# Rows of V at 160 bytes instead of 130, value matmuls of 66 columns, and the mask's key pattern in a shared buffer

## The chip, the core and the metric

The kernel runs on one core of one Trainium2 chip. The metric is the device time of one launch in microseconds; lower is better.

## The reference

Two layers, one behind the other: attention with a block mask, and a gated feed-forward network (FFN) with RMS normalisation.

```python
# q, k, v: (4, 8, 768, 64) float32; blocks of 32, 24 blocks
scores = q @ k.T / sqrt(64)
mask = neighbouring blocks | first and last block (rows and columns) | 3 sampled blocks per row block
attn = softmax(where(mask, scores, -1e9))
x = (attn @ v), heads side by side        # (3072, 512)
xn = x / sqrt(mean(x * x) + 1e-6) * rms_g
out = (silu(xn @ w_gate) * (xn @ w_val)) @ w_out   # d_ff 1536
```

## The kernel before, in words

**Groups.** The 3072 tokens are worked through in nine groups of token tiles of 128: batch 0 in three groups of two tiles, batches 1 to 3 in two groups of three tiles each. For each group the loop runs over the 8 heads. A head has two steps:

- `scores` (matmuls in L325): keys times queries into PSUM, keys on the partitions, then one exponential per part on ACT (L328) into `ex` in bf16. The mask is part of the matmul: 64 rows of a head's K and Q, and 24 more rows that hold the key pattern (`kind`) and the query pattern (`qmask`).
- `values` (L336): for each token tile `it` and each of the six key tiles `jt` one matmul with a block of `ex` as the weights and a row of V as the moving operand, summed over `jt` in PSUM. `pv` (or `pv_two` for the first group, which takes two heads at a time) then multiplies the 64 columns by the reciprocal of the column of sums.

The values of a head are issued some heads behind its scores (`late_pv`), so that the exponentials are there.

**V.** `load_v` brings V of two heads to SBUF in float32 (`vraw`), and `cast_v` (L118, on DVE) writes it as bf16 into `Vp`, one of two tiles, by the parity of the batch. A partition of `Vp` holds 8 x 6 rows of `VW` = 65 elements: 64 of V, and a one that L204 sets once at the start, so that column 64 of the product is the sum of the exponentials. The rows lie end to end, 130 bytes each: row 6 h + jt belongs to head h and key tile jt.

**FFN.** When a group's attention is done, its rows are normalised and turned, and its FFN is cut into pieces (`ffn_pieces`: `gate` L436, `val` L447, `down` L464). `position()` puts them between the steps of the next group's heads at a fixed rate, so PE has matmuls of both at any time. The products of gate and value go to `hps`, which has two buffers in turn. The last group's FFN has no attention beside it.

**Batch changes.** K and Q of batch 0 are transposed on PE (L288). From batch 1 on they are transposed by DMA: `turn` (L301, into `turned`) and `place` (L310, into `KT` and `QT`), both issued on SP's queue, where the stores of the output (L471) are too.

**The mask's key pattern.** `ki_i` (L185, 32 x 768 int32) is written by GpSimd at the start. `mask_keys` (L224) reads it twice in the opening and turns it into `kind`.

**What sets the order.** Everything is issued in the order in which the Python code emits it; there is no scheduler that reorders. Waits between engines follow from the tiles.

Of the kernel before, what the change touches and what calls it, by code (L numbers as in the profile page):

```python
# [10 lines left out]
BF16 = mybir.dt.bfloat16  # L11
I32 = mybir.dt.int32
# [6 lines left out]
def kernel(  # L19
# [18 lines left out]
    P = 128  # L38
    B, H, S, D = q.shape
    NB = S // 32  # L40
    NC = S // P
# [12 lines left out]
    FIRST = NC // 2  # L54
    KR = D + NB
    NP = H // 2
    VW = D + 1

    ctx.enter_context(tc.manual_schedule())

    const = ctx.enter_context(tc.tile_pool(name="const", bufs=1))
    persist = ctx.enter_context(tc.tile_pool(name="persist", bufs=1))
    ld = ctx.enter_context(tc.tile_pool(name="ld", bufs=1))
    work = ctx.enter_context(tc.tile_pool(name="work", bufs=1))
# [19 lines left out]
    def load_one(b, pr, store):  # L84
        src, name = (k, "kbf") if store is kbf else (q, "qbf")
        t = ld.tile([P, 2, NC * D], BF16, name=name, tag=name, bufs=4)
        nc.gpsimd.dma_start(  # L87
            out=t,
            in_=src[b, 2 * pr:2 * pr + 2].rearrange("e (p c) d -> p e (c d)", p=P))
        store[(b, pr)] = t  # L90
# [21 lines left out]

    KT = [persist.tile([P, H, S], BF16, name=f"KT{i}") for i in range(2)]
    QT = [persist.tile([P, H, S], BF16, name=f"QT{i}") for i in range(2)]
    Vp = [persist.tile([P, H, NC, VW], BF16, name=f"Vp{i}") for i in range(2)]

    def cast_v(b, pr, eng):
        eng.tensor_copy(  # L118
# [63 lines left out]
    ident32 = const.tile([P, P], FP32, name="ident32")  # L182
    make_identity(nc, ident32)
    load_one(0, 1, kbf)
    ki_i = const.tile([32, S], I32, name="ki_i")  # L185
    nc.gpsimd.iota(ki_i[0:NB, :], pattern=[[1, NC], [NC, P]], base=0,
                   channel_multiplier=-32)
    for pr in range(NP):
# [14 lines left out]
    for i in range(2):  # L203
        nc.vector.memset(Vp[i][:, :, :, D:VW], 1.0)  # L204
    kc = const.tile([32, 1], FP32, name="kc")
# [126 lines left out]
    def values(grp, h, ex, op):  # L332
        b, c0, n = grp
        for it in range(n):
            for jt in range(NC):
                nc.tensor.matmul(  # L336
                    out=op[:, it, 0:VW], lhsT=ex[:, jt, it * P:(it + 1) * P],
                    rhs=Vp[b % 2][:, h, jt, :], start=(jt == 0), stop=(jt == NC - 1))

    def pv(grp, h, ex, stage):  # L340
        n = grp[2]
        op = ps_o.tile([P, HC, 80], FP32, name="op", tag="ot")
        values(grp, h, ex, op)
        rz = work.tile([P, HC], FP32, name="rz", tag="rz", bufs=2)
        nc.vector.reciprocal(out=rz[:, 0:n], in_=op[:, 0:n, D])  # L345
        nc.vector.tensor_tensor(  # L346
            out=stage[:, 0:n, h * D:(h + 1) * D], in0=op[:, 0:n, 0:D],
            in1=rz[:, 0:n].unsqueeze(2).to_broadcast([P, n, D]), op=ALU.mult)
# [3 lines left out]
    def pv_two(grp, h, ex, stage):  # L352

        if h % 2 == 0:
            pair_op[0] = ps_o.tile([P, 2, 2, 80], FP32, name="op2", tag="ot")
        op = pair_op[0]
        values(grp, h, ex, op[:, h % 2])
        if h % 2 == 0:
            return
        rz = work.tile([P, 2, 2], FP32, name="rz2", tag="rz2", bufs=2)  # L360
        nc.vector.reciprocal(out=rz, in_=op[:, :, :, D])
        nc.vector.tensor_tensor(  # L362
            out=stage[:, 0:2, (h - 1) * D:(h + 1) * D].rearrange("p c (e d) -> p e c d", e=2),
            in0=op[:, :, :, 0:D], in1=rz.unsqueeze(3).to_broadcast([P, 2, 2, D]), op=ALU.mult)
# [318 lines left out]
    for gi, grp in enumerate(groups):  # L683
        if gi == 0:
            continue
        b, c0, n = grp
# [101 lines left out]
```

## Time and profile before

| what | value |
|---|---|
| time, median of 3 runs | 314.73 us (314.66 to 314.91) |
| span of the profiled execution, first to last instruction | 312.8 us |
| median of the runs above that span | 1.9 us |
| PE busy | 302.8 us, 97% of the span |
| DVE, ACT, POOL busy | 202.7, 205.1 and 52.9 us |
| granted TensorE clock | 1.000 |
| value matmuls (L336) | 1152 |

For the profiled execution the profile gives the span; what lies outside of it is taken from the runs. The page of the profile lists busy times, the costliest groups of instructions by line, and the chain of waits that ended last. PE's matmuls are pipelined and their ends are modelled, so the busy times of groups overlap; the distance from one start to the next is what a matmul takes of PE's time. In the lines, "op<-Vp,ex" names the tile that is written and those that are read, "128x65" the moving operand (partitions x elements), and "idle before" the time in which the engine had nothing to do ahead of it, with what ended it.

### The profile page before, as it was taken

The page shows a single profiled execution, that of the slowest core. Times are in us where ns is not written, and L with a number is a line of the kernel's source. Part 1 is how long each engine was busy: PE and PEld are TensorE (multiplying, and loading weights), DVE is VectorE, ACT ScalarE, POOL GpSimd, SP SyncE. Part 2 cuts the span into 40 slices and gives each one's busy share as a digit, 9 for nine tenths or more (in the row PEclk, how much of TensorE's full clock was granted, in tenths as well). Part 3 has the DMA queues.
Part 4 walks back from the last instruction along what each step waited for, and adds up shares of the span by engine and source line. Part 5 has one row for each costly group of instructions (what it writes and reads, how often), then busy time and mean ns, then how long its engine had stood idle before and what let it go on. Part 6 is the DMA issues. An engine that isn't in the chain of part 4 may idle for free.

```text
span 312.8 us, 7261 instructions
## 1 busy us (share of the span) xinstructions
PE 302.8 (97%) x2850; PEld 201.1 (64%) x2869; DVE 202.7 (65%) x557; ACT 205.1 (66%) x332; POOL 52.9 (17%) x79
## 2 busy tenths in 40 slices
PE   8888999999999999999999999999999999999996
PEld 5666886976787566655666566655666566655653
DVE  6978875775578647682767457683777636674860
ACT  4976775777788586667676766766767567632331
POOL 9935132100220122012010122010000100010000
PEclk9999999999999999999999999999999999999999
DMA  7999999999789469605784277714000130002002
GB/s 166 271 210 208 208 265 142 175 227 136 209 147 162 104 134 158 141 20 146 149 152 101 70 182 127 143 40 119 34 2 0 36 118 2 1 2 101 2 0 102
DMA packets 66730, 36.84 MB, mean 118 GB/s; under 512 B 48308, under 2 KB 62288, under 8 KB 66696
## 3 DMA queue, kind: packets, MB, share of 16 engines
q0 software_dynamic: 16064, 17.90, 31.7%
q1 hardware_dynamic: 50596, 18.47, 27.7%
q8 instruction: 22, 0.36, 0.5%
q14 instruction: 12, 0.10, 0.1%
q10 hardware_dynamic: 36, 0.01, 0.0%
HBM read 28.59 MB, written 6.29 MB: 112 GB/s over the span
## 4 chain that ended last, share of the span: by engine, by line
PE 86%; DMA 7%; ACT 3%; DVE 2%; issue 1%; SPq 1%; ACTq 0%
PE yp L464 19%; PE gp L436 19%; PE vp L447 18%; PE st L325 18%; PE op L336 11%; DMA turned<-qbf 4%; ACT ex L328 2%; DMA QT<-turned 2%; DMA first<-in_q_dram 1%; PE tx L418 0%; DVE QT L293 0%; DVE junk L369 0%; DVE stage L362 0%; PE tqk L288 0%; SPq L133 0%
## 5 line engine op out<-in xcount | busy, mean ns | idle before, releaser
L328 ACT ACTIVATE ex<-st 128x768 bf16<-128x768 f32 x192 | 153.9, 812 | 56.2 <-PE st L325 54.5
L325 PE MATMUL st<-QT,KT 88*128 88x384 bf16 (+1 forms) x432 | 93.5, 308 | 1.9 <-DMA QT<-turned 0.7
L451 DVE SCALAR_TENSOR_TENSOR u<-th,gp 128x384 bf16<-128x384 bf16 (+1 forms) x108 | 54.8, 508 | 40.7 <-ACT th L440 39.0
L436 PE MATMUL gp<-xg,wg 128*128 128x384 bf16 (+1 forms) x432 | 80.7, 307 | 0.0
L447 PE MATMUL vp<-xg,wv 128*128 128x384 bf16 (+1 forms) x432 | 80.2, 307 | 0.4 <-DVE u L451 0.4
L464 PE MATMUL yp<-wo,hps 128*128 128x512 bf16 (+1 forms) x284 | 71.6, 369 | 0.9
L440 ACT ACTIVATE th<-gp 128x384 bf16<-128x384 f32 (+1 forms) x108 | 48.9, 453 | 28.9 <-PE gp L436 28.7
L453 DVE TENSOR_TENSOR hps<-u,vp 128x384 bf16<-128x384 bf16 (+1 forms) x108 | 55.1, 510 | 11.4 <-PE vp L447 0.3
L325 PEld LDWEIGHTS <-KT 88*128 88x128 bf16 x432 | 41.7, 98 | 27.0 <-issue 1.9
L447 PEld LDWEIGHTS <-wv 128*128 128x128 bf16 x432 | 40.6, 97 | 20.9 <-issue 0.6
L436 PEld LDWEIGHTS <-wg 128*128 128x128 bf16 x432 | 40.2, 97 | 20.3
L336 PEld LDWEIGHTS <-ex 128*128 128x128 bf16 x1152 | 46.0, 98 | 11.2 <-DVE stage L362 0.8
L336 PE MATMUL op<-Vp,ex 128*128 128x65 bf16 x1152 | 48.8, 194 | 1.6 <-DVE stage L362 0.5
L464 PEld LDWEIGHTS <-hps 128*128 128x128 bf16 x300 | 27.7, 97 | 22.4
L377 POOL TENSOR_TENSOR rstd<-ssq,mhalf 128x3 f32<-128x3 f32 (+1 forms) x9 | 7.3, 815 | 139.4 <-DVE ssq L369 139.4
L345 DVE RECIPROCAL rz<-op 128x3 f32<-128x3 f32 (+1 forms) x64 | 11.2, 174 | 26.2 <-PE op L336 26.1
L470 ACT ACTIVATE yo<-yp 128x512 f32<-128x512 f32 (+1 forms) x25 | 14.4, 576 | 16.0 <-PE yp L464 16.0
L99 POOL DMA_DIRECT2D vraw<-in_v_dram x16 | 12.0, 753 | 69.4 <-DVE Vp L118 60.4
L346 DVE TENSOR_TENSOR stage<-op,rz 128x192 bf16<-128x192 f32 (+1 forms) x64 | 21.8, 341 | 2.2
L369 DVE CUSTOM_DVE_ANT_0 junk<-stage 128x448 bf16<-128x448 bf16 (+1 forms) x24 | 14.8, 618 | 0.6
L389 DVE SCALAR_TENSOR_TENSOR xs<-stage,rstd,gain 128x512 bf16<-128x512 bf16 x15 | 10.4, 748 | 4.4 <-POOL rstd L377 4.4
L87 POOL DMA_DIRECT2D kbf<-in_k_dram x15 | 11.1, 742 | 7.0 <-DMA wo<-in_moe_w_out_dram 7.0
(73 smaller groups left out, 104.6 us busy)
## 6 DMA issues: line engine op xcount, KB each, us to landing
vraw<-in_v_dram POOLq DMA_DIRECT2D x16, 384.0 KB, 5.1
out_dram<-yo SPq DMA_DIRECT2D x23, 256.0 KB, 2.2
kbf<-in_k_dram POOLq DMA_DIRECT2D x15, 192.0 KB, 5.8
qbf<-in_q_dram POOLq DMA_DIRECT2D x12, 192.0 KB, 6.0
KT<-turned SPq DMA_DIRECT2D x24, 96.0 KB, 4.2
QT<-turned SPq DMA_DIRECT2D x24, 96.0 KB, 2.3
wo<-in_moe_w_out_dram POOLq DMA_DIRECT2D x1, 1536.0 KB, 20.5
wg<-in_moe_w_gate_dram POOLq DMA_DIRECT2D x2, 384.0 KB, 9.8
```

Of the source, the lines that this page charges most:

```text
L325: nc.tensor.matmul(out=at[:, e, 0:tg], lhsT=KT[b % 2][0:KR, h, jt * P:(jt + 1) * P], rhs=QT[b % 2][0:KR, h, c0 * P:c0 * P + tg], start=Tru ...
L328: nc.scalar.activation(out=ex[:, nj * part:nj * (part + 1), :], in_=at[:, 0:nj, 0:tg], func=AF.Exp, scale=SCALE)
L336: nc.tensor.matmul(out=op[:, it, 0:VW], lhsT=ex[:, jt, it * P:(it + 1) * P], rhs=Vp[b % 2][:, h, jt, :], start=(jt == 0), stop=(jt == NC - 1))
L346: nc.vector.tensor_tensor(out=stage[:, 0:n, h * D:(h + 1) * D], in0=op[:, 0:n, 0:D], in1=rz[:, 0:n].unsqueeze(2).to_broadcast([P, n, D]), ...
L369: nc.vector.tensor_tensor_reduce(out=junk[:, 0:hi - lo], in0=part, in1=part, scale=1.0, scalar=(e["ssq"][:, it:it + 1] if lo else DM * 1e- ...
L436: nc.tensor.matmul(out=gp[:, 0:tg], lhsT=wg[:, c, f * P:(f + 1) * P], rhs=xg[:, c, 0:tg], start=(c == 0), stop=(c == KD - 1))
L440: nc.scalar.activation(out=th[:, 0:tg], in_=gp[:, 0:tg], func=AF.Tanh, scale=0.5)
L447: nc.tensor.matmul(out=vp[:, 0:tg], lhsT=wv[:, c, f * P:(f + 1) * P], rhs=xg[:, c, 0:tg], start=(c == 0), stop=(c == KD - 1))
L451: nc.vector.scalar_tensor_tensor(out=u[:, 0:tg], in0=th[:, 0:tg], scalar=1.0, in1=gp[:, 0:tg], op0=ALU.add, op1=ALU.mult)
L453: nc.vector.tensor_tensor(out=hps[:, f, 0:tg], in0=u[:, 0:tg], in1=vp[:, 0:tg], op=ALU.mult)
L464: nc.tensor.matmul(out=yp, lhsT=hps[:, f, tt * P:(tt + 1) * P], rhs=wo[:, f, lo:hi], start=(f == 0), stop=(f == NF - 1))
L470: nc.scalar.mul(out=yo, in_=yp, mul=0.5)
```

## The change

Three things are done:

- The rows of `Vp` are laid 80 elements (160 bytes) apart instead of 65 (130 bytes). Each of the two tiles grows from 6240 to 7680 bytes per partition (48 rows).
- `VW` is 66: two columns of ones are set, and the value matmuls take 66 columns. The second column of sums is not read.
- `ki_i` no longer has a tile of its own; it takes one of the two buffers of `hps`.

```diff
     NP = H // 2
-    VW = D + 1
+    VW = D + 2
+    VS = D + 16
...
-    Vp = [persist.tile([P, H, NC, VW], BF16, name=f"Vp{i}") for i in range(2)]
+    Vp = [persist.tile([P, H, NC, VS], BF16, name=f"Vp{i}") for i in range(2)]
...
-    ki_i = const.tile([32, S], I32, name="ki_i")
+    ki_i = work.tile([32, S], I32, name="ki_i", tag="hps", bufs=2)
     nc.gpsimd.iota(ki_i[0:NB, :], pattern=[[1, NC], [NC, P]], base=0,
                    channel_multiplier=-32)
...
                 nc.tensor.matmul(
                     out=op[:, it, 0:VW], lhsT=ex[:, jt, it * P:(it + 1) * P],
-                    rhs=Vp[b % 2][:, h, jt, :], start=(jt == 0), stop=(jt == NC - 1))
+                    rhs=Vp[b % 2][:, h, jt, 0:VW], start=(jt == 0), stop=(jt == NC - 1))
```

## The prediction

> **What bounds the kernel now.** I read the page's list of busy times first, then the windows by stage, the waits of PE, the chain of waits, and last the timeline and the single records of the value matmuls.
>
> The profiled execution spans 312.8 us. The three runs have a median of 314.73 us, so about 1.9 us lie outside the span; the change touches nothing there. I make the sum against the span and take the difference over to the median.
>
> ```profile
> ## 1 busy us (share of the span) xinstructions
> PE 302.8 (97%) x2850; PEld 201.1 (64%) x2869; DVE 202.7 (65%) x557; ACT 205.1 (66%) x332; POOL 52.9 (17%) x79
> ...
> L336 PE MATMUL op<-Vp,ex 128*128 128x65 bf16 x1152 | 48.8, 194 | 1.6 <-DVE stage L362 0.5
> ```
>
> PE is the bound; DVE and ACT have a third of the span free. The group that the change touches has 1152 matmuls. Its mean of 194 ns is no price, since matmuls overlap: what a matmul costs is the distance from its start to the next start. The windows (PE, PEld, DVE, ACT and POOL busy, clock, DMA share) show where PE time is the kernel's time:
>
> ```profile
> 0.00:26.00 26.00, 21.95 (x241) 16.13 (x243) 20.41 (x69) 18.75 (x28) 19.03 (x34) 1.00 1.11 214
> 26.00:68.40 42.40, 41.17 (x471) 33.87 (x474) 30.76 (x98) 29.66 (x52) 10.51 (x15) 1.00 1.24 203
> 68.40:280.00 211.60, 209.99 (x1959) 134.03 (x1973) 135.47 (x358) 147.10 (x234) 22.52 (x30) 1.00 0.48 100
> ```
>
> From 68.4 to 280 us PE is idle for 1.6 us of 211.6: here a nanosecond off a PE instruction is a nanosecond off the end. The clock is 1.00 throughout. Before 68.4 us the DMA engines are saturated (share above 1), and the chain of waits (start, length, what) goes through them into the first scores of batch 1:
>
> ```profile
> 50.27 0.60 PE yp L464 x3
> 50.87 11.18 DMA turned<-qbf
> 62.04 0.02 issue
> 62.06 0.59 SPq L310
> 62.65 0.05 issue
> 62.70 5.67 DMA QT<-turned
> 68.38 0.25 issue
> 68.62 0.48 PE st L325 x2
> ```
>
> PE waits only 0.7 us there ("PE st L325 <- DMA QT<-turned"), so PE and DMA arrive nearly together. Time saved on PE before this point may just lengthen that wait.
>
> Now the value matmuls themselves: one head of a three-tile group is 18 of them, with the next instruction behind. Two heads in the timeline:
>
> ```profile
> 143.44 0.74 PE L336 MATMUL op<-Vp,ex 128*128 128x65 bf16 x18
> 144.01 0.38 PE L464 MATMUL yp<-wo,hps 128*128 128x512 bf16 x1
> ...
> 152.41 0.74 PE L336 MATMUL op<-Vp,ex 128*128 128x65 bf16 x18
> 152.99 0.33 PE L447 MATMUL vp<-xg,wv 128*128 128x384 bf16 x1
> ```
>
> Start to next instruction is 0.57 us for the first (head 1) and 0.58 us for the second (head 3). In the single records' start times, in ns, this small difference holds for every batch: heads 1, 2, 5 and 6 take 573 to 575, heads 0, 3, 4 and 7 580 to 583. The code does the same for each; only where the row of V starts differs. Row r = 6 h + jt starts at byte 130 r, which is a multiple of 16 when r is a multiple of 8: r = 8, 16, 32 and 40 (heads 1, 2, 5, 6; jt 2 or 4), and r = 0 and 24, which are jt 0. Sorting the distances of undisturbed records:
> - jt above 0 on such a row: 29.2 on average (96 records);
> - jt 0, on whatever row: 29.5 (192);
> - the matmul right behind jt 0: 34.0 (192); right behind an aligned row: 33.6 (78);
> - all others: 32.5 (443), or 33.0 where r is 7 modulo 8 (78).
>
> The mean over all undisturbed distances is 32.1, over those after 68 us 32.07. A fixed part plus the columns explains the fast ones: 128 columns (the transposes) are 55.6 apart, 384 are 162, 512 are 215.5, which is columns / 2.4 plus some 2.2; 65 columns give 29.3. So about 3 ns of each ordinary value matmul come from where its row lies.
>
> **The change, part by part.** The order of instructions on every engine, and every wait, is the same in the two kernels; only the column count, the places in memory and one shape of a memset differ.
>
> *Rows 160 bytes apart.* 160 is a multiple of 16 and the Vp tiles start on one too (or row 0 modulo 8 would not be the fast one), so all 48 rows of both buffers become aligned, and no row shares 16 bytes with its neighbour. The nearest row of the trace is the aligned one: 29.2 ns. It bounds the cost from below. From above: an aligned row's follower pays 33.6 instead of 32.5, so an aligned row and its follower together save 65.0 - 62.8 = 2.2, not 3.3; if that belongs to the gain, the new distance is 32.5 - 2.2 = 30.3. I take 29.2, because the followers are aligned too and the extra appears only where the follower is not.
>
> *66 columns.* One column is 1 / 2.4 = 0.4 ns by the spacing rows above, so 29.6 (with the other bound 30.7). Below zero is excluded only loosely; the lower end leaves the column out: 29.2.
>
> *The sum on PE.* After 68.4 us there are 48 heads of 18: 864 x (32.07 - 29.6) = 2.13 us, all on the bound. Before it there are 288: 288 x (32.2 - 29.6) = 0.75 us. The chain there goes through many value matmuls up to 50 us, but the transpose DMA then needs 11.18 us in a saturated queue, and I cannot tell whether it lands earlier when issued earlier. Ends: 0 and 0.75; I take half, 0.37.
>
> *Two columns of ones.* Two memsets of 96 instead of 48 elements. They take 98 ns now; the 256-element memset of L165 takes 270, so (270 - 98) / 208 = 0.83 ns per element and 0.04 us more each. The cover is the wait of DVE behind them: it stands 0.77 us before 2.90 us for the DMA of samp_i (shown here), so the cost is nothing, 0.08 us without that cover.
>
> ```profile
> 1.27 0.10 DVE L204 MEMSET Vp<- 128x48 bf16 x1
> 1.49 0.10 DVE L204 MEMSET Vp<- 128x48 bf16 x1
> ...
> 2.90 0.80 DVE L232 SCALAR_TENSOR_TENSOR bm<-samp_i,kc,bm 24x24 f32<-24x24 int32 x3 [0.77 <-DMA samp_i<-in_sampled_blocks_dram]
> ```
>
> *The casts into Vp.* L118, 16 times 554 ns for 768 elements; only the pitch of what they write changes. Between no change and 768 ns plus a fixed part near 0.15 (one element per ns or so): 0 to 0.37 us each. Twelve of them are off the path, beside an engine that is a third idle; the first four lie in the opening, where the chain names one of them (0.48 us at 17.62). I take 0; 4 x 0.37 = 1.5 us is the far end, part of which the DMA-bound stretch before 68 us would hide.
>
> *ki_i in the buffer of hps.* The mask's pattern is read for the last time at 5.9 us (L224), and the FFN writes its first products after 28 us, into the other buffer of the pair; no wait is added, and what would be late next does not exist. Zero.
>
> The sum: 314.73 - 2.13 - 0.37 = 312.2 us.
>
> **The rivals.**
>
> *Borrowed time.* The fast matmul's saving is partly paid by the next. For: 34.0 and 33.6 behind every fast one. Against: the pair still comes out ahead, and behind jt 0 the rows are never aligned. With 30.7: 864 x 1.37 = 1.2 us and nothing from the opening: 313.5.
>
> *Only lone elements cost.* A row could pay 3.3 ns only when one of its 16-byte pieces holds a single element: with 65 columns rows 0 modulo 8 (last piece) and 7 modulo 8 (first piece), 12 of 48. The new rows have none, so 288 x 3.3 = 0.95 us go and the column brings 1152 x 0.42 = 0.48: 314.3. Against: rows 0 modulo 8 are the fastest of all. For: rows 7 modulo 8 are 0.5 above the rest. The Trainium skill (Advanced Engine Details and Errata, SBUF Cachelines) has this rule: lines of 16 bytes, at least two hits needed on each to hide the access. By that rule the change gains half a microsecond, not two and a half; the trace agrees for one kind of row and contradicts it for the other.
>
> *No gain from the rows.* Something else, such as the weight load that comes with each matmul, sets the spacing, and alignment went with it by chance; or the rows do not lie where I think. Then the extra column is all: +0.48 us, 315.2. The Trainium skill (TensorE: Matmul & The Clock Gate, Back-to-back issue gap) says the pair of weight load and matmul sets the spacing and gives 81 ns at 128 columns; by that the rows could not matter. The trace has 55.6 there, with a load for each, and 29.2 for aligned rows, so a load fits into 29.
>
> *The jump costs: slower.* In the kernel before, consecutive rows touch; the address jumps only back to jt 0, and the matmul after that is the slowest kind, 34.0. If a break between rows is what is paid, at 160 bytes every row has one: 34.0 + 0.4, 2.3 more on 1152, +2.7 us: 317.4. It decides the sign from a spacing of 32.6 upward (0.63 us over 1152). Against: the aligned rows that follow their neighbour without a jump also have a slow follower, and the jump itself costs jt 0 nothing.
>
> **How the numbers follow.** About 0.2% (0.63 us) is what a measurement of this kernel can tell from no change. The forecast gets 0.76: the fast rows are many, in both buffers and every batch, and PE is the bound. Borrowed time 0.09, lone elements 0.05, no gain 0.04, slower 0.06. Faster: 0.76 + 0.09 = 0.85. Same: 0.09 (314.3 and 315.2 are both within 0.63). Slower: 0.06. Range: down to 1152 x 2.87 = 3.3 us of gain (spacing 29.2, the opening's whole gain), 311.4; up past borrowed time to the edge of what counts as faster, 314.1.
>
> **What would show it.** In the changed kernel's timeline, a head of 18 value matmuls should take 0.53 to 0.54 us to the next instruction, the same for every head (0.55 with borrowed time, 0.58 or more without a gain, 0.62 for the jump). The wait of the scores for QT<-turned should grow from 0.7 towards 1.4 us as far as the opening's gain is lost. The memsets should take some 0.14 us, the casts stay at 0.55. The step that I trust least is the half for the opening; the forecast falls if the heads stay at 0.57 us.

## The result, and the profile after

| | median, us | runs |
|---|---|---|
| kernel before | 314.40 (313.67 to 315.09) | 22 |
| changed kernel | 313.16 (312.36 to 321.04) | 22 |

The ratio is 0.9968, with a 95% interval of 0.9956 to 0.9981: 1.0 us faster by the ratio, 1.2 by the medians. The run of 321.04 us was in a slower state and is left out of the ratio. The direction was forecast, the size was not: 312.2 us were predicted.

The profile shown here is of a run of 314.14 us, span 312.4 us. Its value matmuls in the page's list of groups (busy time, mean ns; idle time before):

```profile
L337 PE MATMUL op<-Vp,ex 128*128 128x66 bf16 x1152 | 47.5, 194 | 1.4 <-DVE stage L363 0.5
```

The busy time is 1.3 us less than before, with a mean that did not move: it is the time of one matmul from start to end, 194 ns, while the next ones start some 30 ns apart. The timeline has the spacing, here for heads 1 and 2 of a three-tile group:

```profile
143.80 0.71 PE L337 MATMUL op<-Vp,ex 128*128 128x66 bf16 x18
144.35 0.81 PE L465 MATMUL yp<-wo,hps 128*128 128x512 bf16 x3
...
148.58 0.71 PE L337 MATMUL op<-Vp,ex 128*128 128x66 bf16 x18
149.12 0.81 PE L448 MATMUL vp<-xg,wv 128*128 128x384 bf16 x4
```

Start to next instruction is 0.54 to 0.55 us where it was 0.57 and 0.58. In the single records every head takes 548 or 549 ns, whatever the head: the pattern by head and row is gone. But 548 / 18 is 30.45 ns and not 29.6. The distances are no longer 29, 32.5 and 34, they are 29 (or 30) and 35, with four of 35 in nearly every 18 (45 of the 48 heads), at places that change from head to head.

From the first value matmul of batch 1 to the end the two profiles take 239.12 and 237.86 us. Adding up the distances on PE by line over this stretch, the value matmuls fall from 29.56 to 28.19 us, by 1.37; gate, value and down matmuls stay within 0.02, the scores and transposes give 0.09 back. So the stretch that PE bounds gains what its value matmuls gain, and little else moved.

The opening is another matter. The waits of PE:

```profile
PE tqk L289 <- DMA kbf<-in_k_dram: 1.6, 1, 1.6
PE unread L173 <- DVE idle L166: 1.2, 1, 1.2
```

and the transposes of the second pair of K in the timeline:

```profile
10.87 0.51 PE L289 MATMUL tqk<-ident,kbf 128*128 128x128 bf16 x6 [1.64 <-DMA kbf<-in_k_dram]
```

They started at 9.97 us before:

```profile
9.97 0.51 PE L288 MATMUL tqk<-ident,kbf 128*128 128x128 bf16 x6 [0.58 <-ACT ex L328]
```

The wait for QT<-turned at the batch change, 0.7 us before, is not in this profile: PE came later than the DMA. The first value matmul of batch 1 starts at 74.49 us against 73.69, so this execution had lost 0.8 us by then and more than won it back behind. Its granted clock was 0.93 over the first 26 us, 1.00 from there to 280.

### The profile page after: what moved, and what is told of

It reads as the page before. It is cut to its first block, busy times and chain, and to the rows that moved or that the text cites. A ratio compares the mean times of both kernels' runs of the same rounds, so it can differ in the third digit from the quotient of the medians.

```text
span 312.4 us, 7261 instructions
## 1 busy us (share of the span) xinstructions
PE 302.2 (97%) x2850; PEld 200.2 (64%) x2869; DVE 202.6 (65%) x557; ACT 205.2 (66%) x332; POOL 53.0 (17%) x79
## 4 chain that ended last, share of the span: by engine, by line
PE 92%; DMA 2%; DVE 2%; ACT 1%; POOL 1%; issue 1%; POOLq 0%; ACTq 0%
PE gp L437 20%; PE vp L448 20%; PE yp L465 20%; PE st L326 19%; PE op L337 11%; DMA kbf<-in_k_dram 2%; ACT ex L329 1%; PE tx L419 1%; PE tqk L289 1%; DVE junk L370 0%; DVE stage L363 0%; PE unread L173 0%; POOL kbf L88 0%; POOL ki_i L187 0%; DVE QT L294 0%
## 5 line engine op out<-in xcount | busy, mean ns | idle before, releaser
L454 DVE TENSOR_TENSOR hps<-u,vp 128x384 bf16<-128x384 bf16 (+1 forms) x108 | 55.0, 510 | 11.4 <-PE vp L448 0.3
L337 PEld LDWEIGHTS <-ex 128*128 128x128 bf16 x1152 | 45.0, 98 | 10.9 <-DVE stage L363 0.8
L337 PE MATMUL op<-Vp,ex 128*128 128x66 bf16 x1152 | 47.5, 194 | 1.4 <-DVE stage L363 0.5
```

Of the source, the lines that this page charges most:

```text
L337: nc.tensor.matmul(out=op[:, it, 0:VW], lhsT=ex[:, jt, it * P:(it + 1) * P], rhs=Vp[b % 2][:, h, jt, 0:VW], start=(jt == 0), stop=(jt == N ...
L454: nc.vector.tensor_tensor(out=hps[:, f, 0:tg], in0=u[:, 0:tg], in1=vp[:, 0:tg], op=ALU.mult)
```

## The experiments

Theories: *alignment* (the forecast's: a row not at a multiple of 16 bytes is slow) against *shared line* (a row is slow when its first 16 bytes hold the end of the row read just before). In the changed kernel both are cured. Beside that, two questions: what makes 30.45 out of 29.6, and where the opening's gain is. "Head" is 18 value matmuls of a three-tile group, start to next start, median by head. Diffs are against the changed kernel unless they say otherwise.

### Aligned or apart

Rows at 146 bytes: at the same places modulo 16 as before, but apart.

```diff
-    VW = D + 2
-    VS = D + 16
+    VW = D + 1
+    VS = D + 9
```

> 65 columns, rows at 146 bytes: each row starts at the same place modulo 16 as in the kernel before (146 and 130 both leave 2), but no two rows share 16 bytes. Theory 'alignment' (a row that does not start at a multiple of 16 costs 3 ns): heads of 573 and 581 ns as before, 314.4 us, ratio 1.000. Theory 'shared line' (a row costs more where its first 16 bytes hold the end of the row read just before): about 548 ns for every head, 313.2 us, ratio 0.997.

Ratio 0.9950 (0.9932 to 0.9968), 312.89 us, heads of 550 to 554 ns:

```profile
141.92 0.71 PE L337 MATMUL op<-Vp,ex 128*128 128x65 bf16 x18
142.47 0.81 PE L465 MATMUL yp<-wo,hps 128*128 128x512 bf16 x3
```

42 of the 48 rows are as unaligned as before, and the gain is there, with heads 2 to 6 ns longer than the 548 of the changed kernel. Alignment falls.

The order alone, in the kernel before, with no memory moved:

```diff
-            for jt in range(NC):
+            for jt in (0, 2, 4, 1, 3, 5):
```

> The kernel before with one thing changed: the six key tiles are summed in the order 0, 2, 4, 1, 3, 5, so no row of V is read right behind the row that it touches; 65 columns, 130 bytes, no memory moved. Theory 'shared line' (a row costs 3 ns more where its first 16 bytes hold the end of the row read just before): heads of about 548 to 552 ns as at 146 and 160 bytes, ratio to the kernel before 0.995 to 0.997, about 313 us. Rival 'layout' (rows that touch are slow whatever the order, by where they lie): heads of 573 to 583 ns as before, ratio 1.000.

Ratio 0.9953 (0.9939 to 0.9966), 312.75 us, heads of 547 to 552 ns:

```profile
142.01 0.71 PE L336 MATMUL op<-Vp,ex 128*128 128x65 bf16 x18
142.56 0.81 PE L464 MATMUL yp<-wo,hps 128*128 128x512 bf16 x3
```

The rows still touch; they are just not read one behind the other. So it is the order of reading over touching rows that costs, and five numbers in a loop do the work of the changed layout. How large the shared piece is, rows of 132 bytes tell:

```diff
-    VS = D + 16
+    VS = D + 2
```

> 66 columns, rows end to end at 132 bytes, in order. 132 leaves 4 modulo 16, so each fourth row starts 16 bytes of its own and the rest share theirs with the row read before. Theory 'shared line': in every head one row above jt 0 is free of it (jt 4 in even heads, 2 in odd ones), so all heads take what heads 1, 2, 5 and 6 took before, 573 to 576 ns (579 if the column costs 0.4 in the slow rows); 0.2 us or less below the kernel before. Rival 'odd rows' (what costs is a start off 4 bytes, which no row has here): 548, as at 160 bytes.

Heads of 567 to 571 ns, ratio 0.9980 (0.9970 to 0.9989):

```profile
143.17 0.73 PE L337 MATMUL op<-Vp,ex 128*128 128x66 bf16 x18
143.74 0.81 PE L465 MATMUL yp<-wo,hps 128*128 128x512 bf16 x3
```

Each fourth row starts at a multiple of 16, and those rows above jt 0 take 29.17 ns (144 records); the others, those at 8 modulo 16 among them, 32.6 to 32.8, and 33.5 right behind jt 0. Starts off 4 bytes are not the cause, and pieces of 8 would have made each second row fast. Pieces of 32 are out too: half of the fast rows start at 16 modulo 32, so they share such a piece with the row read before, and they take 29.1 like the other half. The heads are some 5 ns below what I expected; the row behind a free one takes 32.8 here and not 33.6, and the row behind jt 0 takes 33.5 and not 34.0.

### What 30.45 is made of

The width of the value matmuls at 160 bytes, VW changed alone (with 34 and with 64 columns part of the product is left out, as the texts say):

> 65 columns, rows at 160 bytes: the changed kernel without the second column of ones. In the changed kernel a head of 18 value matmuls takes 548 ns, 30.45 each, whatever the head: distances of 29 with four of 35. Theory 'pair floor' (a weight load and its matmul together cannot follow faster than 30.45 on average): again 548 ns per head, the same time as the changed kernel, 313.2 us, ratio to the kernel before 0.996 to 0.997. Theory 'columns' (columns / 2.4 plus a fixed 2.95 ns): 30.03 each, 541 ns per head, 0.4 us less than the changed kernel. Theory 'even columns' (an odd count costs in itself): over 548 ns.

> 34 columns at 160 bytes in all groups but the first: half of V's columns are left out of the value matmuls (the other half is written twice, so VectorE's work stays). Theory 'pair floor': 30.45 each, 548 ns per head as with 66 columns, 313.2 us. Theory 'columns': 34 / 2.4 + 2.95 = 17.1, or a floor lower than 30.45 in between; at 25 each a head takes 450 ns and the time falls by (864 + 192) x 5.4 = 5.7 us.

> 80 columns at 160 bytes (16 of ones). Theory 'pair floor': the columns bind above the floor, 80 / 2.4 + 2.2 = 35.5 each and no distances that stand out by 6 ns, 639 ns per head, 864 x 5.05 = 4.4 us over the changed kernel, up to 5.8 with the opening. Theory 'columns': 80 / 2.4 + 2.95 = 36.3 with some distances 6 ns longer, 653 ns per head, 5.0 to 6.7 us more.

> 72 columns at 160 bytes. So far heads of 18 took 458 ns with 34 columns (25.4 each), 548 with 65 and with 66 (30.45), 642 with 80 (35.7). Theory 'whole lines' (a row is read in pieces of 16 bytes, eight columns, and 65 to 72 columns cost nine pieces): 548 again, the time of the changed kernel. Theory 'columns with a rest' (columns / 2.4 plus 2.3, with some 1 ns lost at 65 and 66 for a reason of their own): 32.3 each, 581 per head, 864 x 1.8 = 1.6 us over the changed kernel.

> 64 columns at 160 bytes: the column of ones is left out of the value matmuls (the last column of V stands in for the sum). Theory 'whole lines': eight pieces instead of nine, a jump down from 30.45 by about 3 ns, to 27 or 28 each, 490 to 505 per head, 2.2 us below the changed kernel. Theory 'columns with a rest': 64 / 2.4 + 2.3 = 29.0 at best and 30.45 at most, 522 to 548 per head, 0 to 1.3 us below.

> 68 columns at 160 bytes (four of ones). Heads of 18 took 523 ns with 64 columns, 548 with 65 and with 66, 582 with 72, 642 with 80. 64, 72 and 80 fit columns / 2.4 plus 2.35 (29.0, 32.35, 35.7). Theory 'steps of four' (the columns are taken in fours, 65 to 68 cost the same): 548 again, as with 65 and 66. Theory 'steps of two' (with some 0.5 ns of its own at 65 and 66): 68 / 2.4 + 2.35 = 30.7, 552 per head or more, up to 560.

| columns | head, ns | each, ns | columns / 2.4 + 2.35 | ratio to before |
|---|---|---|---|---|
| 34 | 454 to 458 | 25.3 | 16.5 | 0.9819 (0.9781 to 0.9856) |
| 64 | 524 | 29.1 | 29.0 | 0.9933 (0.9915 to 0.9952) |
| 65 | 548 | 30.45 | 29.4 | 0.9948 (0.9925 to 0.9970) |
| 66 | 548 | 30.45 | 29.85 | 0.9968 (0.9956 to 0.9981) |
| 68 | 560 | 31.1 | 30.7 | 0.9988 (0.9967 to 1.0010) |
| 72 | 582 | 32.3 | 32.35 | 1.0020 (0.9999 to 1.0040) |
| 80 | 642 | 35.7 | 35.7 | 1.0129 (1.0096 to 1.0162) |

The page's group of the kernel with 80 columns beside that with 64, where the busy time follows the width:

```profile
L337 PE MATMUL op<-Vp,ex 128*128 128x80 bf16 x1152 | 53.3, 202 | 1.5 <-DVE stage L363 0.5
```

```profile
L337 PE MATMUL op<-Vp,ex 128*128 128x64 bf16 x1152 | 45.5, 193 | 1.4 <-DVE stage L363 0.5
```

"Pair floor" falls: with 34 columns a weight load and its matmul follow each other in 25.3 ns, so a load as such fits into much less than 30.45. "Whole lines" falls at 72 (32.3, not 30.45) and "steps of four" at 68 (560, not 548). A straight line through 64, 72 and 80 explains the size of the column's price; 65, 66 and 68 lie 0.4 to 1.0 ns above it, by distances that stand out by 6 ns: four in 18 with 65 and 66, three with 68, none with 64, 72 and 80. The distances between the long ones lie below the line (29.2 with 65 and with 66, 30.0 with 68), so the long ones are all of the excess. It is 48 x 18 x 0.6 = 0.5 us of what the changed kernel was to gain behind the opening. What sets these distances I did not find. The second column of ones costs nothing in the heads (548 with either) and brings nothing; the intervals of the two ratios, 0.9948 and 0.9968, overlap.

The Trainium skill (TensorE: Matmul & The Clock Gate, Back-to-back issue gap) gives some 60 cycles, 25 ns, as the least distance for narrow matmuls. The trace agrees at 34 columns (25.3); at 64, which that table puts in the same class, it has 29.1.

### The opening

The changed kernel again:

> The changed kernel once more, for a profile without the wait of 1.6 us for the first kbf and the clock's dip behind it. From the first value matmul of batch 1 to the end it took 237.9 us against 239.1 before; that should come again within 0.2. If the opening's gain of some 0.5 us arrives (24 groups of 12 matmuls at 1.7 ns less), that point is reached at 73.2 us or earlier (73.7 before); if the DMA takes it back, at 73.7 or later. Time 312.5 to 313.2.

Ratio 0.9970 (0.9952 to 0.9987), 313.24 us; first value matmul of the kernel at 11.76 us (11.09 before), of batch 1 at 73.75, from there 238.38 us. That is 0.5 us more than the 237.86 that should have come again. The single records show where: the gate matmul at 110.43 us starts 0.66 us after the score ahead of it, where 0.16 is usual, and the timeline puts the wait down to the DMA of `xg`. The value matmuls take 548 ns per head again.

Then ki_i's buffer alone, in the kernel before (this diff is against it):

```diff
-    ki_i = const.tile([32, S], I32, name="ki_i")
+    ki_i = work.tile([32, S], I32, name="ki_i", tag="hps", bufs=2)
```

> Only ki_i in the buffer of hps, V as before (65 columns, 130 bytes). No wait is added, so theory and rival of the rows both say the time of the kernel before, heads of 573 and 581 ns, ratio 1.000. Theory 'opening' (the shared buffer, or the tiles that move up in memory by 3072 bytes, delay the first loads): first value matmul after 11.5 us instead of 11.1, ratio 1.001 to 1.002.

Ratio 1.0013 (0.9990 to 1.0036), first value matmul at 11.06 us, heads of 571 to 583: the shared buffer costs nothing that these runs can tell. By then the late openings (11.4 to 12.0 us) were all in kernels whose load tiles do not start at a multiple of 512 bytes, and a theory of placement looked good, though one kernel of that kind, with 64 columns, was early (11.07). Rows at 146 bytes in tiles of the changed size moved them off:

```diff
+    Vp = [persist.tile([P, H * NC * (D + 16)], BF16, name=f"Vp{i}")[:, 0:H * NC * VS].rearrange(
+        "p (h c d) -> p h c d", h=H, d=VS) for i in range(2)]
```

> Rows at 146 bytes as in the earlier run (which had 312.9 us and its first value matmul at 11.1 us), but Vp's tiles are as large as in the changed kernel, so that all tiles behind them lie where they lie there. The two profiles of the changed kernel have the first value matmul at 11.8 and 12.0 us. Theory 'placement' (the later opening comes from where the loads' tiles lie): 11.6 us or later and 313.2 us. Theory 'chance' (loads under contention land within a microsecond or so of each other from run to run): 11.1 to 12 us with no pattern, median 312.7 to 313.2. Heads of 550 to 554 ns in either.

11.97 us, ratio 0.9979 (0.9959 to 0.9998), 313.37 us: for placement, it seemed. So unused bytes were put behind Vp, in the changed kernel (back onto multiples of 512) and behind the old rows (off them), and the order alone was run again:

```diff
+    pad = persist.tile([P, 96], BF16, name="pad")      # 1440 in the second kernel
```

> The changed kernel with 192 unused bytes behind Vp, so that the tiles of the loads (q0, kbf, qbf, vraw, first) lie at the same addresses as in the kernel before, all multiples of 512. Theory 'placement' (loads into tiles off a multiple of 512 bytes land later under contention): first value matmul at 11.1 us, median about 312.7 us, ratio 0.995, 0.4 us better than the changed kernel. Theory 'chance': 11.1 to 12 us, 313.2 us, ratio 0.997. Heads of 548 ns in either.

> The rows of the kernel before (65 columns, 130 bytes), ki_i in the buffer of hps, and 2880 unused bytes behind Vp, so that the tiles of the loads lie at the same addresses as in the changed kernel, 320 bytes past a multiple of 512. Theory 'placement': first value matmul at 11.6 us or later, 314.7 to 315 us, ratio 1.001 to 1.002. Theory 'chance': as the kernel before, ratio 1.000. Heads of 573 and 581 ns in either.

> The kernel before with the key tiles in the order 0, 2, 4, 1, 3, 5, once more, beside the padded versions on the same chip: 312.7 us, ratio 0.995 to 0.996, first value matmul at 11.1 us by 'placement' (its load tiles are where the kernel before has them), anywhere from 11.1 to 12 by 'chance'.

| kernel | load tiles | first value matmul, us | ratio |
|---|---|---|---|
| changed, padded by 192 | on 512 | 11.77 | 0.9943 (0.9920 to 0.9967) |
| old rows, padded by 2880 | off | 11.33 | 1.0000 (0.9983 to 1.0018) |
| order alone, again | on 512 | 11.78 | 0.9945 (0.9921 to 0.9970) |

The order alone had 11.06 us in its first profile and has 11.78 here, from the same code on another chip:

```profile
9.83 0.50 PE L288 MATMUL tqk<-ident,kbf 128*128 128x128 bf16 x6
11.34 0.28 PE L288 MATMUL tqk<-ident,q 128*128 128x128 bf16 x2
11.78 0.53 PE L336 MATMUL op<-Vp,ex 128*128 128x65 bf16 x12
```

A late load is not what delayed this one: the second `kbf` landed at 9.48 us, and at 9.59 in the first profile. PE's pace differs. The first six scores, in the first profile and here:

```profile
5.82 0.91 PE L325 MATMUL st<-QT,KT 88*128 88x256 bf16 x6
```

```profile
5.78 1.49 PE L325 MATMUL st<-QT,KT 88*128 88x256 bf16 x6
```

In the single records, matmuls of 256 columns start 213 ns apart at first and 109 ns apart later; the change comes at 6.0 us in the first profile and at 7.1 us here. The clock in the windows is 1.00 in both and does not show it. From these scores the delay passes through copies on DVE (L162, L255, L293) to the scores ahead of the first value matmul.

In the changed kernel padded by 192 a load is late, though on 512: q of the second pair landed at 11.27 us, against 9.98 and 10.17 in the two profiles of the order alone. So the first value matmul does not decide about placement. The landings as a whole speak for it: the last load of V of batch 0 lands at 15.6 to 16.1 us in the six profiles with load tiles on 512, and at 16.0 to 18.0 us in the eleven off it, and on each of the three chips of the experiments every one off it is later than every one on it. What this costs in time is not shown. The ratios without padding and with it are 0.9968 and 0.9970 against 0.9943 with the changed rows (padding puts them on 512), 0.9950 against 0.9979 with rows at 146 bytes and 1.0013 against 1.0000 with the old rows (padding puts these two off it); in each case the intervals overlap.

Over the profiles, the first value matmul of batch 1 starts at 73.1, 73.4 and 73.7 us with the old rows (mean 73.4), and with rows apart or out of order (65 or 66 columns) at 72.5 to 74.5, mean of eight 73.3: 72.9 for the four on 512 and 73.7 for the four off it. With this spread they show neither that the opening's gain of 0.5 us arrives nor that it does not.

## Why the prediction was right or wrong

- *PE bounds the stretch behind the batch change, a nanosecond there is one at the end*: right. 1.37 us fewer in value matmuls, 1.26 us off the stretch; the other profiles of kernels with fast rows take 237.9 to 238.0 us for it, but 238.4 in the second of the changed kernel, with its wait of 0.5 us for `xg`, and those with the old rows 239.1.
- *29.2 ns for a row by itself, because it is aligned*: the reading failed. The fast rows above jt 0 are those that start 16 bytes of their own; they are aligned, but their alignment is not why, and rows of jt 0 are fast because the row read before them is not their neighbour. The sorting by "r a multiple of 8" could not tell the two apart, and the text took the name of the one. The remark that no new row shares 16 bytes with its neighbour named the condition that counts.
- *A spacing of 29.6*: the term that was mis-sized. It is 30.45 to 30.5; 864 x (32.07 - 30.5) = 1.36 instead of 2.13 us. The step that failed is the choice of 29.2 over 30.3, with the reason that the extra appears only where the follower of a fast row is not aligned: here all rows are aligned, and four distances of 18 are 35. Single rows of 29.2 stood between rows of 32.5; a whole head of such rows does not hold 29.2 at this width. The bound of 30.7 that the text kept was nearer than its value, and so was the rival of borrowed time with its 313.5 us and its sign of 0.55 us per head, which is what the timeline has. Its account was wrong in part: it is not the follower of each fast row that pays, but four of 18 wherever they fall; why, stays open.
- *0.4 for the 66th column*: wrong here. Between 65 and 66 it is 0; from 72 to 80 a column costs the 0.42 that was worked out (35.7 - 32.3 over 8).
- *Half of the opening, 0.37*: not seen in the changed kernel, whose two profiles reach the first value matmul of batch 1 at 74.49 and 73.75 us against 73.69. The wait for QT<-turned, which was to grow as the gain is lost, is absent from the first and 0.6 us in the second, so it is not what took the gain. The prediction put the moved places in memory at nothing; with load tiles off 512 the last load of V landed later, as told above. Whether that takes the 0.37 stays open.
- *Memsets, casts, ki_i at nothing*: right as far as measured. The memsets take 138 ns, as worked out, and DVE still waits for samp_i behind them, 0.90 us; the casts take 560 ns on average (557 before); with ki_i's buffer alone the ratio is 1.0013, not clear of 1.
- *Lone elements*: fell. With 65 columns at 160 bytes each row leaves one element alone in its last 16 bytes, and the head takes the same 548 ns. The Trainium skill (Advanced Engine Details and Errata, SBUF Cachelines) has lines of 16 bytes and puts the price on those with fewer than two hits; the runs show pieces of 16 bytes, but the price on a piece that the read just before ended in.
- *No gain from the rows*: fell, since the order of reading alone, with the same columns and bytes, gives 0.9953.
- *The jump costs*: fell, since each row at 160 bytes follows a jump.

With 1.36 for the spacing and 0 for the opening the sum is 313.4 us from the 314.73 of the prediction, and 313.0 from 314.40, the median of the 22 runs before. The median measured is 313.16.

## What to carry to other kernels

When a small matmul is repeated over rows that lie end to end, look at single start-to-start distances sorted by row before padding anything: here reading the rows in another order, with no byte moved, gave 0.9953 and 0.9945, which is as good as the padded layout within the intervals (0.9968 and 0.9970). And a cheap case that occurs alone among dear ones is a lower bound, not the price of many in a row: measure it in a row, or keep the nearest bound that contains what its neighbours pay.

## What the runs showed of the hardware that was not expected

- A moving row that begins in the 16 bytes in which the previous matmul's row ended costs 3.3 ns more (32.5 against 29.2 with 65 columns); pieces of 8 or of 32 bytes do not fit the records with rows of 132 bytes.
- The spacing of matmuls that each load new weights of 128 columns is 25.3 ns at 34 columns, 29.1 at 64 and 35.7 at 80; at 65, 66 and 68 it is 0.4 to 1.0 ns above the line through 64, 72 and 80, in single steps of 6 ns, cause open.
- In two executions of the same code, on two chips, matmuls of 256 columns started 213 ns apart until 6.0 us in the one and until 7.1 us in the other, and 109 ns apart behind that; the first value matmul moved from 11.06 to 11.78 us. The clock in the windows is 1.00 in both.
